# A fused attention and expert kernel: the first transfers in another order, the sink products a tick later, and one copy on another engine

## The chip, the cores and the metric

The kernel runs on one core of a Trainium2 chip. The metric is the device time of one execution in microseconds; three executions of the kernel before took 293.79, 293.94 and 297.29 us, and their median, 293.94 us, is the time before.

## The reference: what is computed

Attention with 4 batches, 8 heads, 768 positions and 64 channels per head, in which a query sees the first 4 positions (the sinks) and the last 128 positions; then a top-1 mixture of 8 experts, each of which serves at most 80 tokens. Cut to what matters:

```
scores = q @ k.T / 8;  keep = (key < 4) | (0 <= query - key < 128)
a = softmax(where(keep, scores, -1e9));  x = (a @ v) as 3072 rows of 512
logits = x @ w_gate;  expert = argmax;  gate_w = softmax(logits)[expert]
for e in 8 experts: keep the 80 tokens of e with the largest gate_w
    out[tok] = gate_w * (relu(x[tok] @ w1[e]) @ w2[e]);  all other rows are 0
```

## The kernel before, in words

**Engines and tiles.** Attention runs in 48 ticks (the loop at L987). A tick handles two units; a unit is one block of 128 queries of one pair of heads. In the first four ticks the units are blocks 0 and 1 of head pairs 0, 1, 2 and 3 of the first batch. TensorE computes the scores (`scores`, L566, matmuls at L581) into one of two PSUM banks, one for each unit, which the next tick uses again. VectorE masks them and takes the maxima (`softmax`, L590: L599, L602, L604, L609). ScalarE takes the exponentials (`exps`, L612: L619) and so frees the bank. GpSimd sorts out the sink columns (`sink_probs`, L622: L627, L628), TensorE turns the probabilities (`transposes`, L635) and the sink columns (`sinks_turn`, L639), ScalarE copies both out (`keep_probs` L646, `sinks_keep` L642), GpSimd cuts the triangles (L654, L661), and TensorE multiplies by the values (`weighted_sinks` L673, `weighted` L687). A tick issues the scores of tick n, the turning of n-1 and the weighted sums of n-2.

**The gate's logits inside the values.** Each head's 64 value columns are followed by 8 columns that hold v times w_gate, so the weighted sum also gives the gate's logits. `value_logits` (L425, matmuls at L433) computes these columns from the turned values `vt` and the gate weights `wg`, and `value_keep` (L436, the copy at L439) writes them into the tile of values `vv`, over zeros that the transfer of `vv` has brought; so it has to come after that transfer. `sink_logits` (L441, L447) and `sink_keep` (L450, L452) do the same for the values of the sinks, from `sv_cols` into `vst_raw`. `round_v` (L412) and `split_v` (L416) then round the sink values for TensorE, one head pair in each of ticks 1 to 4, on VectorE.

**Order.** The ticks are in a hand-written order (`manual_schedule`, L980): each engine executes its instructions in the order of the program text. Work outside the fixed steps is put into named slots by `at(...)` (L875) and comes out at `run(...)`: in a tick, "pe front" comes after the scores and ahead of the turning of the tick before; "pe mid" after the VectorE steps; "act mid" after the exponentials and ahead of `keep_probs`; "pe end" ahead of the weighted sums; "dve end" last, in the order of the `at` calls. One spare PSUM bank (`misc`, L706) is used by turn: the warm-up matmuls of tick 1 (L985), the turned sink columns, then the value logits; each waits until the copy that empties it is done.

**The first transfers.** All are issued by SyncE's queue, in program order. Their sizes are 128 KB for each pair of queries (`first_q`, L467), 132 KB for each pair of keys (`first_k`, L468), 32 KB for `wg`, 256 KB for `sv_cols`, 288 KB for `vst_raw`, 512 KB for `vt`, 576 KB for the first two blocks of `vv`, and 512 KB for the queries of the second group of ticks (`load_q(1)`, L382). Before the change the order is: pair 0 (queries, keys), pair 1, `wg`, `sv_cols`, `vv`, `vt`, pair 2, `vst_raw`, pair 3, `load_q(1)`. GpSimd scales each pair of queries by 0.125 (`scale_first`, L485): pairs 0 and 1 ahead of the ticks, pair 2 in tick 0 and pair 3 in tick 1, each ahead of that tick's `sink_probs`. The queries of the second group are scaled in tick 2 (`scale_q`, L458).

After attention the 24 blocks of tokens are ranked by their gate weights, the rows of the chosen tokens are gathered, and the experts' two matmuls run to the end (L1239, L1260).

Of the kernel before, what the change touches and what calls it, by code (L numbers as in the profile page):

```python
# [26 lines left out]
NPAIR = H // 2  # L27
# [217 lines left out]
def attention_moe(ctx: ExitStack, tc, q, k, v, n_sink, window, w_gate, w1, w2, capacity, q_t, k_t, v_t, vt_t, vs_t, sv_t, wg_t, out):  # L245
    nc = tc.nc
    ve, ac, po, pe = nc.vector, nc.scalar, nc.gpsimd, nc.tensor
# [73 lines left out]
    with ExitStack() as actx:  # L321
# [43 lines left out]
        vst_raw = sm.tile([SROWS, 2, NPAIR, 2 * VD], F32, name="vst_raw", bufs=1)  # L365
# [55 lines left out]
        def load_vt(g):  # L421
            vts[g] = ld.tile([P, NPAIR, 2 * P], F32, tag="vt", name=f"vt_{g}", bufs=1)
            nc.sync.dma_start(vts[g], vt_t[g // NPB, g % NPB])
# [40 lines left out]
        wg = const.tile([P, NPAIR, 2 * E], F32, name="wg")  # L464

        def first_pair(i):
            nc.sync.dma_start(first_q[:, i], q_t[0, 0][:, i])  # L467
            nc.sync.dma_start(first_k[:, i, 0:2 * BLKW], k_t[0][:, i, 0:2 * BLKW])  # L468

        first_pair(0)  # L470
        first_pair(1)
        nc.sync.dma_start(wg, wg_t)
        nc.sync.dma_start(sv_cols, sv_t[0])
        nc.sync.dma_start(vv[0][:, 0:2], v_t[0][:, 0:2])
        load_vt(0)
        first_pair(2)
        nc.sync.dma_start(vst_raw, vs_t[0])
        first_pair(3)
        vst[0], v_done[0] = vst_rows[0], 1
        load_q(1)  # L480
        nc.sync.dma_start(first_k[:, :, 2 * BLKW:4 * BLKW], k_t[0][:, :, 2 * BLKW:4 * BLKW])
# [393 lines left out]
        def at(n, f, *args):  # L875
            cal.setdefault(n, []).append((f, args))
# [51 lines left out]
        at(2, load_v, 0, 3)  # L928
        at((0, "pool"), scale_first, 2)
        at((1, "pool"), scale_first, 3)  # L930
        at((0, "pe end"), sink_logits, 0)
        at((1, "pe end"), sink_keep, 0, ve.tensor_copy)
        for m in range(4):
            at((1 + m, "dve end"), round_v, 0, m, ve.tensor_copy)
            at((1 + m, "dve end"), split_v, 0, m, ve)
        at((1, "pe mid"), value_logits, 0, 0)
        at((1, "pe mid"), value_logits, 0, 1)
        at((1, "act mid"), value_keep, 0)
        for g in range(1, NG):
            n = 4 if g == 1 else 4 * g - 2  # L940
            at((n, "pe front"), value_logits, g, 0)
# [38 lines left out]
        with tc.manual_schedule():  # L980
# [61 lines left out]
            t, i, l = NTK - 1, NTILE - 1, NTILE - 2  # L1042
# [348 lines left out]
```

## Time and profile before

| what | value |
|---|---|
| median of the three executions | 293.94 us |
| profiled execution, its own time | 294.47 us |
| its span, first to last instruction | 292.8 us |
| mean granted TensorE clock | 0.985 of full speed |
| busy share of the span: TensorE matmuls, weight loads | 91%, 74% |
| VectorE, ScalarE, GpSimd | 56%, 58%, 48% |

The profiled execution took 0.53 us more than the median. Of its time 292.8 us lie between the first and the last instruction, and 1.67 us around them. The busy share of TensorE is an average over the whole span; in the first 20 us, which the change touches, TensorE has gaps.

### The profile page before, as it was taken

What the parts mean: (1) busy time and instruction counts of PE and PEld (TensorE: products, weight loads), DVE (VectorE), ACT (ScalarE), POOL (GpSimd) and SP (SyncE); (2) the same over time, 40 slices, a digit from 0 to 9 for tenths busy, and PEclk for the clock granted to TensorE, in tenths of its full rate; (3) what the DMA queues carried; (4) which work ended last, traced back from release to release, by engine and by line L of the source; (5) the groups of instructions that cost most, each with busy time, mean ns of one, the idle gap of its engine ahead of it and who ended that gap; (6) DMA issues with size and microseconds to landing.
All of it is one profiled execution on the core that took longest, in us unless ns stands there. A gap on an engine that the chain in (4) does not pass through costs nothing.

```text
span 292.8 us, 13306 instructions
## 1 busy us (share of the span) xinstructions
PE 266.1 (91%) x5435; PEld 217.9 (74%) x5435; DVE 162.6 (56%) x502; ACT 169.5 (58%) x663; POOL 140.8 (48%) x366
## 2 busy tenths in 40 slices
PE   6699999999999989999989988987979999999991
PEld 2467787777787767777767767555979999999981
DVE  7487858697587968869879888932111011100000
ACT  2377677887868789898989898920102122202220
POOL 4256557755588846657876765847111011011111
PEclk9989999999999999999999999997999999999998
DMA  6997986094964499999999999906996767868501
GB/s 201 318 369 252 320 358 234 3 344 161 341 243 141 130 396 373 344 410 400 354 327 404 324 400 402 386 13 213 281 346 235 255 228 265 296 206 297 181 12 55
DMA packets 30388, 79.18 MB, mean 270 GB/s; under 512 B 3056, under 2 KB 5104, under 8 KB 30320
## 3 DMA queue, kind: packets, MB, share of 16 engines
q1 hardware_dynamic: 29008, 74.85, 71.8%
q0 software_dynamic: 1024, 2.81, 3.3%
q8 instruction: 45, 0.74, 1.0%
q10 hardware_dynamic: 288, 0.60, 0.5%
q14 instruction: 23, 0.19, 0.2%
HBM read 63.46 MB, written 14.78 MB: 267 GB/s over the span
## 4 chain that ended last, share of the span: by engine, by line
PE 55%; ACT 12%; DVE 11%; issue 7%; POOL 7%; DMA 5%; SPq 1%; POOLq 0%; ACTq 0%; DVEq 0%
PE ph L1239 13%; PE py L1260 13%; PE xp L687 7%; PE sc L581 7%; ACT prob L619 7%; PE pp L635 5%; DMA sv_cols<-in_sv_t_dram 4%; PE vw L433 3%; DVE sc L602 3%; DVE nm L609 3%; ACT gts L846 2%; POOL pt L661 1%; DMA xg<-x_rows,idx_in 1%; PE ts L639 1%; PE pry L1298 1%
## 5 line engine op out<-in xcount | busy, mean ns | idle before, releaser
L619 ACT ACTIVATE prob<-sc,nm 128x132 f32<-128x132 f32 (+1 forms) x192 | 69.5, 370 | 21.1 <-DVE nm L609 14.7
L581 PE MATMUL sc<-kv,q 64*64 64x196 f32 (+2 forms) x768 | 45.9, 334 | 4.0 <-ACT prob L619 3.6
L602 DVE COPY_PREDICATED sc<-upper,sc 128x256 f32<-128x256 int8 x80 | 33.8, 423 | 21.9 <-PE sc L581 11.0
L609 DVE TENSOR_REDUCE nm<-sc 128x2 f32<-128x264 f32 (+1 forms) x96 | 41.4, 431 | 3.3
L687 PE MATMUL xp<-kv,pt 128*64 128x72 f32 x752 | 41.0, 229 | 0.7 <-POOL pt L661 0.2
L1300 POOL DMA_INDIRECT out_dram<-y,idx x8 | 7.4, 922 | 65.6 <-ACT y L1299 55.3
L619 ACT ACTIVATION_READ_ACCUMULATOR prob<-sc,nm 128x1 f32 x192 | 38.7, 202 | 0.0
L1223 DVE COPY xs<-px 128x320 f32<-128x320 f32 x8 | 3.9, 492 | 57.0 <-PE px L1221 56.5
L687 PE MATMUL xp<-kv,own 128*64 128x72 f32 x624 | 34.4, 231 | 0.0
L581 PEld LDWEIGHTS sc<-kv,q 64*64 64x64 f32 x768 | 22.4, 133 | 15.4 <-ACT prob L619 9.6
L687 PEld LDWEIGHTS xp<-kv,pt 128*64 128x64 f32 x752 | 31.0, 137 | 3.1 <-POOL pt L661 1.1
L635 PE MATMUL pp<-ident,prob 128*128 128x128 f32 x192 | 31.5, 287 | 0.9 <-ACT pt L646 0.9
L627 POOL CAST stk<-prob 128x32 fp32r<-128x32 f32 x48 | 11.3, 235 | 43.3 <-ACT prob L619 39.3
L1243 ACT ACTIVATE h<-ph 128x320 f32<-128x320 f32 x16 | 7.0, 437 | 38.2 <-PE ph L1239 38.2
L661 POOL TENSOR_SCALAR_AFFINE_SELECT pt<-pt 128x512 f32<-128x512 f32 (+1 forms) x48 | 27.2, 566 | 3.3
L646 ACT COPY pt<-pp 128x512 f32<-128x512 f32 x48 | 28.0, 584 | 0.5 <-POOL own L654 0.5
L654 POOL TENSOR_SCALAR_AFFINE_SELECT own<-pt 128x512 f32<-128x512 f32 (+1 forms) x48 | 27.2, 567 | 0.6 <-ACT pt L646 0.6
L635 PEld LDWEIGHTS pp<-ident,prob 128*128 128x128 f32 x192 | 20.8, 143 | 8.8 <-ACT pt L646 5.3
L687 PEld LDWEIGHTS xp<-kv,own 128*64 128x64 f32 x624 | 25.6, 137 | 2.2
L846 ACT ACTIVATE gts<-krow,under 128x768 bf16<-128x768 f32 x24 | 22.7, 946 | 0.5 <-ACT ex L745 0.2
L1239 PE MATMUL ph<-xs,w 128*64 128x80 f32 x512 | 20.4, 241 | 1.1 <-DVE xs L1223 0.6
L1239 PEld LDWEIGHTS ph<-xs,w 128*64 128x64 f32 x512 | 19.7, 144 | 1.4 <-DVE xs L1223 0.7
(178 smaller groups left out, 510.2 us busy)
## 6 DMA issues: line engine op xcount, KB each, us to landing
w<-in_moe_w_dram SPq DMA_DIRECT2D x16, 1024.0 KB, 8.4
kv<-in_v_t_dram SPq DMA_DIRECT2D x12, 576.0 KB, 7.3
x_rows<-xr SPq DMA_DIRECT2D x22, 292.0 KB, 3.9
vt<-in_vt_t_dram SPq DMA_DIRECT2D x12, 512.0 KB, 7.0
out_dram<-zeros SPq DMA_DIRECT2D x24, 256.0 KB, 7.7
wkv<-in_moe_w_dram SPq DMA_DIRECT2D x6, 1024.0 KB, 8.4
q<-in_q_t_dram SPq DMA_DIRECT2D x11, 512.0 KB, 7.9
kv<-in_moe_w_dram SPq DMA_DIRECT2D x5, 1024.0 KB, 7.8
```

The lines of the kernel that those rows point to most:

```text
L581: pe.matmul(sc[u * D:(u + 1) * D, h, c0 + lo:c0 + hi], qs[g][r, hp, q0:q0 + D], ks[b][r, hp, k0 + lo:k0 + hi], start=True, stop=True, skip ...
L602: ve.copy_predicated(own, upper, sc[:, :, 0:P])
L609: ve.tensor_reduce(out=nm, in_=sc[:, :, lo_c:hi_c], axis=AX.X, op=ALU.max, negate=True)
L619: ac.activation(prob[:, a, h, p0:], sc[:, h, lo_c:hi_c], AF.Exp, bias=nm[:, h:h + 1], scale=1.0, accum_out=ssum[:, n, 2 * hp + h:2 * hp + ...
L635: pe.transpose(st[(t, "pp")][:, a, h], prob[:, a, h, SINK:], ident)
L646: ac.copy(pt, st.pop((t, "pp")))
L654: po.affine_select(out=own[:, a0:], in_=pt[:, a0:], pattern=[[0, 2 - a0], [0, 2], [1, P]], compare_op=ALU.is_ge, fill=0.0, base=0, channel ...
L661: po.affine_select(out=pt[:, a0:], in_=pt[:, a0:], pattern=[[0, 2 - a0], [0, 2], [-1, P]], compare_op=ALU.is_gt, fill=0.0, base=0, channel ...
L687: pe.matmul(xp[m * D:(m + 1) * D, a, h * VD:(h + 1) * VD], pr[:, a, h, m * D:(m + 1) * D], val[:, (2 * hp + h) * VD:(2 * hp + h + 1) * VD] ...
L846: ac.activation(gt, krow[:, c * PIECE:(c + 1) * PIECE], AF.Sign, bias=under[:, i:i + 1], scale=BELOW, accum_out=ra)
L1239: pe.matmul(ph[fc // (HC // 2)][m * D:(m + 1) * D, fc % (HC // 2)], columns(0, e, c, fc * P + m * D), x[:, c], start=(c == 0 and fc % (HC ...
L1260: pe.matmul(to[m * D:(m + 1) * D, dc], columns(1, e, k, dc * P + m * D), h[:, k], start=(k == 0 and (between is not None or dc == 0)), sto ...
```

## The change

Three edits. The queries and keys of pairs 2 and 3 go ahead of `sv_cols`, and `vt` and `vst_raw` go ahead of `vv`, so that `vv` is the last of these thirteen transfers. The sink products of the first batch move from the end of tick 0 to the "pe front" slot of tick 1. The first value logits are copied out by VectorE at the end of tick 1 (behind `round_v` and `split_v` of that tick, by the order of the `at` calls), no longer by ScalarE in its middle.

```diff
-        first_pair(0)
-        first_pair(1)
-        nc.sync.dma_start(wg, wg_t)
+        for i in range(NPAIR):
+            first_pair(i)
+            if i == 1:
+                nc.sync.dma_start(wg, wg_t)
         nc.sync.dma_start(sv_cols, sv_t[0])
+        load_vt(0)
+        nc.sync.dma_start(vst_raw, vs_t[0])
         nc.sync.dma_start(vv[0][:, 0:2], v_t[0][:, 0:2])
-        load_vt(0)
-        first_pair(2)
-        nc.sync.dma_start(vst_raw, vs_t[0])
-        first_pair(3)
...
-        at((0, "pe end"), sink_logits, 0)
+        at((1, "pe front"), sink_logits, 0)
         at((1, "pe end"), sink_keep, 0, ve.tensor_copy)
...
-        at((1, "act mid"), value_keep, 0)
+        at((1, "dve end"), value_keep, 0, ve.tensor_copy)
```

## Rows read from the trace of the kernel before

**Rows 1.** Waits of TensorE from 40 to 200 us: total us, times, longest us.
```profile
PE sv L447 <- DMA sv_cols<-in_sv_t_dram: 0.3, 1, 0.3
```

**Rows 2.** Busy time by stretch: us, length, engines, granted clock, DMA share, GB/s.
```profile
15.00:16.00 1.00, 1.00 (x15) 0.44 (x8) 0.58 (x2) 0.42 (x1) 0.43 (x2) 0.50 0.99 374
...
22.00:24.00 2.00, 2.00 (x46) 1.62 (x38) 1.93 (x5) 1.07 (x6) 1.77 (x6) 1.00 0.17 63
```

**Rows 3.** Chain that ended last, 0 to 40 us: start, length, what.
```profile
3.13 4.10 DMA sv_cols<-in_sv_t_dram
...
11.73 0.41 POOL q L485
...
12.68 0.31 PE ts L639
...
13.32 1.31 PE vw L433 x32
```

**Rows 4.** Transfers issued in 0 to 4 us: size, us from issue to landing.
```profile
kv<-in_v_t_dram SPq DMA_DIRECT2D x1, 576.0 KB, 5.1
```

**Rows 5.** The same view, those issued in 4 to 8.6 us.
```profile
vt<-in_vt_t_dram SPq DMA_DIRECT2D x1, 512.0 KB, 7.0
q<-in_q_t_dram SPq DMA_DIRECT2D x1, 512.0 KB, 7.9
```

**Rows 6.** SyncE's queue in order of time, 0 to 45 us: start, length, transfer.
```profile
3.60 0.43 SPq L474 DMA_DIRECT2D kv<-in_v_t_dram  x1
4.08 0.43 SPq L423 DMA_DIRECT2D vt<-in_vt_t_dram  x1
...
6.93 0.43 SPq L468 DMA_DIRECT2D kv<-in_k_t_dram  x1
7.41 0.43 SPq L382 DMA_DIRECT2D q<-in_q_t_dram  x1
```

**Rows 7.** Instructions in order of time, 0 to 24 us, all engines; idle before in brackets.
```profile
7.37 1.07 PE L447 MATMUL xp<-wg,sv_cols 128*64 128x16 f32 x16 [1.45 <-DMA sv_cols<-in_sv_t_dram]
...
8.19 0.36 ACT L619 ACTIVATE prob<-sc,nm 128x132 f32<-128x132 f32 x1
...
9.13 0.78 PE L581 MATMUL sc<-kv,q 64*64 64x64 f32 x16
...
9.84 0.66 PE L635 MATMUL pp<-ident,prob 128*128 128x128 f32 x4
...
13.01 0.26 ACT L642 CAST stt<-ts 64x128 fp32r<-64x128 f32 x1 [1.46 <-PE ts L639]
...
13.47 0.28 DVE L452 COPY vst_raw<-xp 64x128 f32<-64x128 f32 x1 [1.76 <-DMA vst_raw<-in_vs_t_dram]
...
13.74 0.41 POOL L485 TENSOR_SCALAR q<-q 128x256 f32<-128x256 f32 x1 [1.07 <-DMA q<-in_q_t_dram]
...
13.79 0.51 DVE L412 CAST vst<-vst_raw 64x288 fp32r<-64x288 f32 x1
...
14.67 0.27 ACT L439 COPY kv<-vw 128x128 f32<-128x128 f32 x1 [0.69 <-PE vw L433]
...
15.39 0.49 DVE L599 COPY_PREDICATED_SCALAR sc<-upper,negc 128x256 f32 x1 [0.61 <-PE sc L581]
...
18.10 0.45 DVE L416 TENSOR_TENSOR vst<-vst_raw,vst 32x288 fp32r<-32x288 f32 x1
...
18.87 0.49 DVE L599 COPY_PREDICATED_SCALAR sc<-upper,negc 128x256 f32 x1 [0.32 <-PE sc L581]
```

**Rows 8.** The same view: the later roundings of sink values, and the scaling beside one.
```profile
16.86 1.05 POOL L458 TENSOR_SCALAR q<-q 128x1024 f32<-128x1024 f32 x1
...
17.32 0.75 DVE L412 CAST vst<-vst_raw 64x288 fp32r<-64x288 f32 x1
...
20.80 0.29 DVE L412 CAST vst<-vst_raw 64x288 fp32r<-64x288 f32 x1
```

**Rows 9.** All transfers of values issued at L402: us to landing, least, median, most.
```profile
DMA to landing us min/median/max: 6.7/8.5/12.1
```

## The prediction

> **What bounds the kernel now.** I read the page's busy shares first, then the waits of TensorE, then the chain of waits over the first 40 us, and last the instructions and SyncE's queue in order of time. From 40 to 200 us TensorE waits for a transfer only once, for 0.3 us [rows 1]: there nothing is tied to the clock on the wall, and a tick that starts earlier should end earlier. The first 20 us are different. The chain runs through the sink columns' transfer, then GpSimd's scaling of pair 2 at 11.73, the turned sink columns at 12.68 and the value logits at 13.32 [rows 3]. The exponentials of tick 0 are over at 8.19 + 0.36 = 8.55 [rows 7], so GpSimd could have begun the sink columns then; it stands behind the scaling of pair 2, whose queries land just before 11.73. That is a stall of 3.2 us, and it is what the new order of the transfers removes. The sink products of tick 0 run at 7.37 [rows 7], beside that stall. VectorE meanwhile waits until 13.47 for the sinks' values [rows 7].
>
> **The change, step by step.** The transfers first. They land in the order of issue, roughly as their bytes add up. By the sizes in the text above: 1384 KB, up to and with the values, are down at 3.60 + 5.1 = 8.70 [rows 4, 6]; 1896 KB, with the turned values, at 4.08 + 7.0 = 11.08 [rows 5, 6]; 2444 KB, with the sinks' values, at 13.47, where VectorE's wait for them ends; 2572 KB, with the queries of pair 3, at 13.74, where GpSimd's does [rows 7]; and 3216 KB at 7.41 + 7.9 = 15.31 [rows 5, 6]. I use this curve for the new order, an assumption that the nearest rows carry: the thirteen first transfers are the same set, issued at the same spacing, so SyncE's issues add nothing.
>
> Pairs 2 and 3 then stand at 680 to 1072 KB and are down before 8.70. GpSimd needs pair 2 ahead of the sink columns of tick 0, at 8.55, and pair 3 a tick later. So both scalings (0.41 us each) cost nothing, covered by GpSimd's wait for the exponentials. If pair 2 came later than 8.1, each us would count as before, up to the 3.2 us.
>
> What is late next on TensorE: the scores of tick 1 need the banks that the exponentials free, the second at 8.55; the second half of the 0.78 us [rows 7] puts their end at 8.94. The sink columns' products stand right behind, in front of the turning. Their transfer is at 1328 KB, so down by 8.70, and TensorE does not wait for it; the products cost 1.07 us, now on TensorE's path, to 10.01. The turning takes 0.66 [rows 7], to 10.67, the turned sink columns 0.31 [rows 3], to 10.98, their copy 0.26 [rows 7], to 11.24. The value logits wait for that copy, since it empties the bank, and for the turned values: 1840 KB, 11.1 by the curve. They take 1.31 [rows 3] and end at 12.55. Before they end at 13.32 + 1.31 = 14.63. So TensorE is 2.1 us ahead here.
>
> VectorE does not follow by as much. Its copy of the sink logits waits for the sinks' values, now at 2128 KB: 11.08 + 232/548 of 2.39 = 12.09. The copy 0.28, the rounding 0.51 and the split 0.45 (the duration of the later one) [rows 7] bring it to 13.33, 13.4 with the gaps. Then comes the new work, `value_keep`. Its duration is in no row on this engine: 0.27 on ScalarE, 0.28 for the nearest copy out of PSUM on VectorE with half the partitions [rows 7]. I take 0.28. ScalarE gets 0.27 back, which is worth nothing here, since its next exponentials wait for VectorE's maxima.
>
> The new wait is the point. `value_keep` writes over what the transfer of `vv` brings, and that transfer is now the thirteenth, at 2704 KB: by the curve 13.74 + 132/644 of 1.57 = 14.06. ScalarE did not feel it before, because the values were down at 8.70. So VectorE stands until 14.06 and ends the copy at 14.34. Queued behind it on VectorE are the masks and maxima of tick 2; for those wait the exponentials, and for these the banks of tick 3. TensorE's turned sink columns of tick 1 wait for the same copy, to get the spare bank. The mask of tick 2 starts at 14.36 in place of 15.39 [rows 7]: 1.03 us are left of the 2.1.
>
> From that mask to the one of tick 3, VectorE's own work took 18.10 + 0.45 - 15.39 = 3.16 us; then it waited 0.32 for the scores, to 18.87 [rows 7]. TensorE was slow there: the granted clock was 0.50 between 15 and 16 us [rows 2], the level of 1.2 GHz, after it had stood still from 10.5 to 12.68. In the new order TensorE is done with the value logits 1.5 us before VectorE is ready, so even at that level it has time, and the 0.32 goes. The mask of tick 3 starts at 14.36 + 3.16 = 17.52, 1.35 us earlier. From there the ticks run as before.
>
> Of this, 3.16 has another end. The rounding of tick 2 took 0.75 us at 17.32, beside GpSimd's scaling from 16.86 to 17.91, and 0.29 us at 20.80 [rows 8]. In the new order the scaling starts when its queries land, 15.31, and ends at 16.36, while the rounding starts at about 16.3 (1.93 after the mask, as before). They may just miss each other, which gives 0.46 more. The Trainium skill (SBUF — State Buffer, section Who interferes with whom) says that VectorE's two-port copies and GpSimd share a pair of ports and that the second to issue waits out the first; by this rule the gain would be 1.35 + 0.46 = 1.81 us, and the two roundings quoted agree with it.
>
> **The sum.** 1.35 us off. The profiled execution took 294.47 and would take 293.1; against the median, 0.53 lower, that is 293.94 - 1.35 = 292.6 us. The landing of `vv` can lie between 13.74 and 15.31 by the rows around it, so this case alone runs from a gain of 1.7 to one of 0.1: 292.2 to 293.8.
>
> **Rivals.** (1) The roundings miss the scaling: 1.81 us, 292.1. For it speak the two durations [rows 8]; against it that the estimate of both times is within 0.1 us of an overlap. (2) `vv` is no wait: it lands by 13.4, and VectorE goes on at 13.4 + 0.28 = 13.7, 0.66 earlier than I have it; 2.0 us, 291.9. For it: the values of a later block took at least 6.7 us [rows 9], which from 6.93, the issue of the thirteenth [rows 6], is 13.63. Against: the bytes ahead of it. (3) The gain is given back later: 293.9. It needs a point in the ticks or behind them that depends on a transfer alone. The queue of transfers runs empty in 22 to 24 us [rows 2], so all that was sent in this stretch is down by then, before the ticks use it; that speaks against, and I know of no such point from the rows. But the order of four engines over 44 more ticks can lose a us in small waits. (4) Slower: `value_keep` holds VectorE longer than the removed stall did. The place is the end of tick 1, the price 1 us for each us that `vv` lands after 14.06 + 1.35 = 15.41. The values at L402 took 8.5 us at the median and 12.1 at most [rows 9], which from 6.93 is 15.43 and 19.03. At the middle of the two, 17.2, it costs 1.8: 295.7. Against it: those were sent when larger transfers were ahead of them, and the fourteenth transfer is down at 15.31.
>
> **How the numbers follow.** The forecast has 0.45, (1) 0.15, (2) 0.1, (3) 0.2, (4) 0.1. The time is 292.6; its own range is 292.2 to 293.8. The range from 291.7 to 294.2 holds the forecast and (1) to (3), with 0.2 us for the scatter of the runs, and leaves out (4) and what the small sizes may miss. A measurement of this kernel can tell 2%, 5.9 us, from no change. None of the cases comes near it: the stall itself is 3.2 us, and the far end of (4), 19.03, costs 3.6. So 0.01 for faster by that much, 0.97 for within, 0.02 for slower.
>
> **What would show it.** In the changed profile GpSimd's scaling of pair 2 has no wait behind 9 us; the sink products stand between 8.9 and 10.1; the value logits end near 12.6; VectorE's longest wait in 11 to 15 us is at the copy at L439, for the transfer of the values, until about 14.1; the mask of tick 2 (the third pair's L599) starts at about 14.4 and that of tick 3 near 17.5, and every later tick is 1.3 us earlier. Wrong would be: a wait for the sink columns or the turned values that lasts on TensorE, no wait at L439, one past 15.4, or ticks that start earlier and end at the old time.

## The result, and the profile after

The changed kernel took 295.34 us at the median of 20 executions, the kernel before 294.42 in as many on the same chip: a ratio of 1.0063 [1.0042, 1.0085], some 1.85 us slower by the ratio and 0.92 by the medians. Ratios leave out single executions more than 1.5% above the fastest of their kernel; medians have all. The forecast was 292.6 us, with a range from 291.7 to 294.2, counted from a median of three executions that lay 0.48 below that of the twenty. So the change cost time where a gain of 1.35 us was forecast, and stayed within the 2% to which the prediction gave 0.97. The profiled execution took 296.68 us: 294.5 from its first to its last instruction (before 292.8) and 2.18 around them (before 1.67), at a mean granted clock of 0.978 (before 0.985). On the page TensorE's matmuls are busy for 268.2 us, VectorE for 161.9, ScalarE for 169.1 and GpSimd for 140.0.

First the chain of waits of the changed kernel over the first 40 us (start, length, what). It answers to [rows 3].

```profile
5.51 6.68 DMA vt<-in_vt_t_dram
12.32 1.89 PE vw L433 x32
14.22 1.29 PE sc L580 x12
```

The sink columns and GpSimd's scaling are gone from the chain; a transfer has taken their place, that of the turned values, until 12.19. Then the instructions of the same trace in order of time (start, length, engine, line, what; the idle time before it and what ended it in brackets), which answer to [rows 7, 8].

```profile
1.12 4.86 PE L490 MATMUL sc<-ones_bf 128*128 128x512 bf16 x12 [1.12 <-DVE ones_bf L262]
...
5.96 0.40 POOL L484 TENSOR_SCALAR q<-q 128x256 f32<-128x256 f32 x1 [1.43 <-DMA q<-in_q_t_dram]
...
9.96 1.10 PE L447 MATMUL xp<-wg,sv_cols 128*64 128x16 f32 x16
...
11.79 0.26 ACT L641 CAST stt<-ts 64x128 fp32r<-64x128 f32 x1 [0.93 <-PE ts L638]
...
12.32 1.89 PE L433 MATMUL vw<-wg,vt 128*64 128x16 f32 x32 [0.57 <-DMA vt<-in_vt_t_dram]
...
13.72 0.28 DVE L452 COPY vst_raw<-xp 64x128 f32<-64x128 f32 x1 [2.39 <-DMA vst_raw<-in_vs_t_dram]
...
14.98 0.29 DVE L439 COPY kv<-vw 128x128 f32<-128x128 f32 x1
15.30 0.49 DVE L598 COPY_PREDICATED_SCALAR sc<-upper,negc 128x256 f32 x1
...
16.23 1.04 POOL L458 TENSOR_SCALAR q<-q 128x1024 f32<-128x1024 f32 x1 [1.22 <-DMA q<-in_q_t_dram]
...
17.23 0.29 DVE L412 CAST vst<-vst_raw 64x288 fp32r<-64x288 f32 x1
...
19.35 0.49 DVE L598 COPY_PREDICATED_SCALAR sc<-upper,negc 128x256 f32 x1 [1.34 <-PE sc L580]
```

The scaling of pair 2 is over at 6.36, and GpSimd's stall is gone. Yet the sinks' values land at 13.72 (13.47 in [rows 7]), though 316 KB fewer stand ahead of them, and the mask of tick 2 starts at 15.30 (15.39). `value_keep` at 14.98 waits for no transfer. The mask of tick 3 starts at 19.35, 0.48 later than before, behind a wait of 1.34 us for scores. The first line is TensorE's warm-up ahead of the ticks, twelve matmuls whose results nobody uses. Before the change it read:

```profile
1.12 4.08 PE L491 MATMUL sc<-ones_bf 128*128 128x512 bf16 x12 [1.12 <-DVE ones_bf L262]
```

It took 0.78 us longer this time, and the scores of tick 0, behind it, started at 5.91 in place of 5.13. Third, the granted clock in the same trace (stretch, length, busy time and count of TensorE, its weight loads, VectorE, ScalarE and GpSimd, then granted clock, DMA share, GB/s), which answers to [rows 2].

```profile
13.00:14.00 1.00, 1.00 (x24) 1.00 (x22) 0.28 (x1) 0.23 (x1) 0.85 (x5) 0.50 0.99 394
...
15.00:16.00 1.00, 1.00 (x9) 0.56 (x4) 0.93 (x3) 0.00 (x0) 0.01 (x1) 0.50 1.12 390
...
18.00:19.00 1.00, 1.00 (x22) 0.86 (x22) 0.01 (x1) 0.95 (x4) 0.68 (x4) 0.50 0.95 352
```

The clock column reads 0.60 from 12 to 13 us and 0.50, the level of 1.2 GHz, from 13 to 19 us. Fourth, why the sinks' values came no earlier. The same columns for 6 to 8 us, before the change:

```profile
6.00:8.00 2.00, 0.63 (x12) 0.67 (x12) 1.63 (x5) 0.98 (x5) 0.00 (x0) 1.00 1.01 392
```

and after it:

```profile
6.00:8.00 2.00, 1.44 (x19) 0.54 (x19) 1.44 (x4) 0.46 (x3) 0.36 (x1) 1.00 0.81 212
```

The last two columns matter. The same queue moved 392 GB/s before and 212 after, with the DMA engines busy 0.81 of the time. 180 GB/s less for 2 us is 0.36 MB, about what the new order had saved ahead of the sinks' values (316 KB).

### The profile page after: what moved, and what is told of

Read it like the earlier page. It is cut to its first block, busy times and chain, and to the rows that moved or that the text cites. A ratio compares the mean times of both kernels' runs of the same rounds, so it can differ in the third digit from the quotient of the medians.

```text
span 294.5 us, 13307 instructions
## 1 busy us (share of the span) xinstructions
PE 268.2 (91%) x5435; PEld 219.4 (74%) x5435; DVE 161.9 (55%) x503; ACT 169.1 (57%) x662; POOL 140.0 (48%) x366
## 4 chain that ended last, share of the span: by engine, by line
PE 56%; ACT 11%; DVE 10%; issue 7%; POOL 7%; DMA 7%; SPq 2%; POOLq 0%; ACTq 0%; DVEq 0%
PE ph L1238 13%; PE py L1259 13%; PE xp L686 8%; ACT prob L618 7%; PE sc L580 7%; PE pp L634 5%; PE vw L433 3%; DMA sv_cols<-in_sv_t_dram 3%; DMA vt<-in_vt_t_dram 2%; DVE sc L601 2%; DVE nm L608 2%; POOL pt L660 2%; ACT pt L645 1%; PE px L1220 1%; POOL own L653 1%
## 5 line engine op out<-in xcount | busy, mean ns | idle before, releaser
L618 ACT ACTIVATE prob<-sc,nm 128x132 f32<-128x132 f32 (+1 forms) x192 | 69.4, 369 | 23.3 <-DVE nm L608 13.5
L580 PEld LDWEIGHTS sc<-kv,q 64*64 64x64 f32 x768 | 22.6, 135 | 18.1 <-ACT prob L618 11.1
L1272 ACT COPY yt<-py 128x320 f32<-128x320 f32 x7 | 3.0, 426 | 30.5 <-PE py L1259 30.5
## 6 DMA issues: line engine op xcount, KB each, us to landing
x_rows<-xr SPq DMA_DIRECT2D x22, 292.0 KB, 4.0
```

The costliest lines, as they stand in the source:

```text
L580: pe.matmul(sc[u * D:(u + 1) * D, h, c0 + lo:c0 + hi], qs[g][r, hp, q0:q0 + D], ks[b][r, hp, k0 + lo:k0 + hi], start=True, stop=True, skip ...
L618: ac.activation(prob[:, a, h, p0:], sc[:, h, lo_c:hi_c], AF.Exp, bias=nm[:, h:h + 1], scale=1.0, accum_out=ssum[:, n, 2 * hp + h:2 * hp + ...
```

## The experiments

Fifteen kernels ran. All ratios are to the kernel before, on the same chip, with a 95% interval.

**The changed kernel again, and each edit alone.** The first kernel is the changed one; the other four keep a part of its diff.

```
all_again:  the whole change
order_only: the new order of the transfers alone
sink_only:  at((1, "pe front"), sink_logits, 0) alone
keep_only:  at((1, "dve end"), value_keep, 0, ve.tensor_copy) alone
order_sink: the first two, without the copy on VectorE
```

> The changed kernel once more. It measured 0.6% slower than before, about 1.9 us. If that comes from the first 20 us (theories below), the ticks should again be late by about 0.5 us at tick 3, with the mask of tick 3 at about 19.3 us in place of 18.87, TensorE's granted clock at 0.50 for longer than in the kernel before (there 14.5 to 17.5 us), and the sinks' values landing near 13.6 us. If the step of 1.25 us between ticks 31 and 34 (a wait of 1.2 us for the sink columns of the last batch) is chance, it is not in this trace, and the time is nearer to 1 us than to 2 us slower.

> The new order of the transfers alone. Theory L (late transfers: the pairs of queries and keys, sent ahead, push sink columns, turned values and sinks' values back more than their bytes say): the sink products, still at the end of tick 0, wait on TensorE for the sink columns until about 9.4 us, the scores of tick 1 end near 11.5, and the kernel is slower than the changed one, by 1 us or more over before. Theory V (the copy of the value logits holds VectorE): with the copy on ScalarE, as fast as before or faster. Theory K (TensorE's clock is at the lower level for longer after its gaps): slower by the longer time at 1.2 GHz, with more idle time on TensorE before 13 us than in the changed kernel.

> The sink products in tick 1 alone, transfers and copy as before. Theories L and V: no change within 0.3 us, since GpSimd still waits for pair 2 until 11.7 us and TensorE's sink columns for GpSimd. Theory K: TensorE's gaps lie elsewhere (about 6.7 to 8.6 us, and 10.6 to 12.7), so the clock may fall earlier or for longer, and then the time is up to 1 us off in step with the length of the stretch at 0.50.

> The copy of the first value logits on VectorE alone, transfers and sink products as before. The values are down at 8.7 us, so VectorE does not wait for them; the copy takes about 0.29 us between the split at 14.3 and the mask at 15.39, where VectorE was idle for 0.61 us. Theories L and K: no change within 0.3 us. Theory V: slower by 0.5 to 1.9 us.

> The new order and the moved sink products, with the copy of the value logits back on ScalarE: the changed kernel without its third edit. The runs so far show 2.1 us around the span for both kernels that have the copy on VectorE and 1.75 us for all others, so here 1.75 us are expected. Theory V (the copy holds VectorE inside the span): span shorter than the changed kernel's by 0.3 us or more at the same granted clock. Theories L and K: the same span at the same clock within 0.3 us, so the whole gain over the changed kernel is the 0.35 us around the span.

| kernel | median us | ratio |
|---|---|---|
| all_again | 296.49 | 1.0039 [1.0000, 1.0079] |
| order_only | 299.93 | 1.0136 [1.0082, 1.0190] |
| sink_only | 296.02 | 0.9999 [0.9960, 1.0038] |
| keep_only | 295.36 | 1.0004 [0.9963, 1.0045] |
| order_sink | 295.55 | 1.0059 [1.0031, 1.0088] |

The new order is the edit that costs: the nine measurements of kernels with pairs 2 and 3 sent ahead of `sv_cols`, the first one and those further down among them, gave ratios of 1.0038 to 1.0136. With the sink products moved as well, 1.0136 becomes 1.0059, on another chip and with intervals that overlap at their ends: that the move takes back part of the loss is likely, and how much is not shown. The copy on VectorE changes nothing that this measurement can tell. In order_only, TensorE's products wait for the sink columns with the scores of tick 1 behind them:

```profile
8.97 1.50 PE L447 MATMUL xp<-wg,sv_cols 128*64 128x16 f32 x16 [1.96 <-DMA sv_cols<-in_sv_t_dram]
...
12.63 0.49 DVE L598 COPY_PREDICATED_SCALAR sc<-upper,negc 128x256 f32 x1 [3.79 <-PE sc L580]
```

That mask is the one of tick 1, after VectorE had waited 3.79 us. In the second trace of the changed kernel the same program looks otherwise than in the first:

```profile
12.18 0.28 DVE L452 COPY vst_raw<-xp 64x128 f32<-64x128 f32 x1 [0.22 <-DMA vst_raw<-in_vs_t_dram]
...
13.90 0.29 DVE L439 COPY kv<-vw 128x128 f32<-128x128 f32 x1 [0.62 <-PE vw L433]
...
14.35 0.49 DVE L598 COPY_PREDICATED_SCALAR sc<-upper,negc 128x256 f32 x1 [0.16 <-PE sc L580]
...
17.14 0.49 DVE L598 COPY_PREDICATED_SCALAR sc<-upper,negc 128x256 f32 x1
```

Here the sinks' values are there at 12.18 and the mask of tick 2 starts at 14.35, as forecast. But the kernel with the old order has such executions too, as keep_only shows:

```profile
12.15 0.28 DVE L452 COPY vst_raw<-xp 64x128 f32<-64x128 f32 x1 [0.98 <-DMA vst_raw<-in_vs_t_dram]
13.53 0.29 DVE L439 COPY kv<-vw 128x128 f32<-128x128 f32 x1
13.85 0.49 DVE L599 COPY_PREDICATED_SCALAR sc<-upper,negc 128x256 f32 x1
```

The landing moves by 1.5 us between executions of one order. So one trace on each side can't show a shift of 1.4 us, and the one of before that I took as the base, with the landing at 13.47, lies at the late end.

**The kernel before, again,** without an edit, for that spread.

> The kernel before, once more. Theory P: its sinks' values land in the range of the traces with its order of transfers, 12.2 to 13.5, and its mask of tick 2 starts 1.3 to 2.1 us later; the trace in which the prediction was read was a late one (13.5 and 15.4). If it is typical, both are within 0.3 us of those again. Ratio 1.00 within 0.4%, which shows what this measurement can tell apart.

It measured 1.0036 [1.0000, 1.0072] against itself (294.63 us): ratios of 0.4% say little here. Its landing and mask:

```profile
13.17 0.28 DVE L452 COPY vst_raw<-xp 64x128 f32<-64x128 f32 x1 [1.92 <-DMA vst_raw<-in_vs_t_dram]
...
14.50 0.49 DVE L599 COPY_PREDICATED_SCALAR sc<-upper,negc 128x256 f32 x1
```

Over six traces with the old order the copy at L452 starts at 12.15 to 13.47, mean 12.88, and the mask of tick 2 at 13.83 to 15.49. Over five with the new order in which that transfer still stands behind the turned values and nothing is merged (the changed kernel's two, order_sink, after_warm and after_act_one_more) it is 12.18 to 13.72, mean 12.90, and 13.91 to 15.30. The landing did not move.

The start of the ticks has a spread too: in the sixteen traces with twelve warm-up matmuls ahead of them, these take 4.06 to 5.30 us, and the scores of tick 0 start at 5.11 to 6.35. The trace of the kernel before, with 5.13, lies at the early end.

**Fewer, larger transfers.** Pairs 2 and 3 of the changed kernel as one transfer of queries and one of keys:

```diff
-        for i in range(NPAIR):
-            first_pair(i)
...
+        nc.sync.dma_start(first_q[:, 2:4], q_t[0, 0][:, 2:4])
+        nc.sync.dma_start(first_k[:, 2:4, 0:2 * BLKW], k_t[0][:, 2:4, 0:2 * BLKW])
```

> The changed kernel, with pairs 2 and 3 sent as one transfer of queries (256 KB) and one of keys (264 KB), two issues fewer. Theory S (SyncE issues one transfer in about 0.47 us, so small ones hand out only some 270 KB per us and the engines that move the data run short): in 4 to 8.6 us 1.3 MB or more are moved in place of 1.02 to 1.18 MB, the sinks' values land 0.7 to 1.2 us earlier (11.3 to 12.8 in place of 12.2 to 13.7), and the mask of tick 2 starts earlier by about as much, 13.0 to 14.3. Theory K (the clock alone): landing times and mask as in the changed kernel, 13.9 to 15.3. Time around the span 2.1 us.

295.75 us, 1.0050 [1.0011, 1.0090]. What moved in 4 to 8.6 us, before the change (packets, MB, mean rate, packets below three sizes):

```profile
DMA packets 595, 1.42 MB, mean 309 GB/s; under 512 B 147, under 2 KB 224, under 8 KB 595
```

after it:

```profile
DMA packets 923, 1.10 MB, mean 239 GB/s; under 512 B 214, under 2 KB 733, under 8 KB 923
```

and with the merged transfers:

```profile
DMA packets 862, 1.29 MB, mean 281 GB/s; under 512 B 206, under 2 KB 503, under 8 KB 862
```

Against the first trace of the changed kernel more than half of the lost bytes come back (1.18 MB in its second trace), and in 6 to 8 us the rate is 326 GB/s in place of 212. So the run of small transfers causes the low rate. Merging takes away two issues and a third of the packets under 2 KB at once; which of the two does it is not told apart. The Trainium skill (DMA: Bandwidth & Descriptors, section Rules for kernel authors) says to join many small transfers into one large one; the three rows agree. The sinks' values landed at 12.89 in this trace, within the spread of both orders: that their landing would come earlier is not shown.

**The sinks' values ahead of the turned values,** with the copy on VectorE (swap) and on ScalarE (swap_act).

```diff
+        nc.sync.dma_start(vst_raw, vs_t[0])
         load_vt(0)
-        nc.sync.dma_start(vst_raw, vs_t[0])
...
-        at((1, "dve end"), value_keep, 0, ve.tensor_copy)
+        at((1, "act mid"), value_keep, 0)
```

> The changed kernel with the transfer of the sinks' values (288 KB) ahead of that of the turned values (512 KB). Theory P (the sinks' values are what VectorE waits for, so their place in the queue sets the mask of tick 2): they land 1 to 2 us earlier than in the changed kernel (10.7 to 12.0 in place of 12.2 to 13.7) and VectorE no longer waits for them, or for less than 1 us. The turned values land up to 1 us later and hold TensorE's value logits instead, so the mask of tick 2 starts at 13.5 to 14.6, earlier than 13.9 to 15.3 by 0.5 us in the mean. Rival K (the clock alone): the time follows the granted clock, and the order of these two changes nothing. Around the span 2.1 us.

> The same with the copy of the value logits on ScalarE as before the change. Around the span 1.75 to 1.8 us in place of 2.1, so faster than the kernel above by 0.3 us from that alone. ScalarE then waits for the values at this copy, ahead of its copy of the turned probabilities; if that holds the ticks up, the span is longer than the kernel's above by 0.3 us or more at the same clock.

swap: 296.60 us, 1.0085 [1.0054, 1.0116]; swap_act: 295.91, 1.0038 [1.0001, 1.0075]. In the trace of swap_act:

```profile
10.92 0.27 DVE L452 COPY vst_raw<-xp 64x128 f32<-64x128 f32 x1
...
13.40 1.11 PE L433 MATMUL vw<-wg,vt 128*64 128x16 f32 x32 [1.96 <-DMA vt<-in_vt_t_dram]
...
14.79 0.27 ACT L439 COPY kv<-vw 128x128 f32<-128x128 f32 x1 [2.34 <-DMA kv<-in_v_t_dram]
15.01 0.49 DVE L598 COPY_PREDICATED_SCALAR sc<-upper,negc 128x256 f32 x1 [3.00 <-PE sc L580]
```

The sinks' values no longer hold anything, and the mask is where it was, not at 13.5 to 14.6 as theory P has it: the value logits now wait 1.96 us for the turned values, and the scores of tick 2 stand behind them. The wait for `vv`, until 14.79 here, is real, but falls on ScalarE. In swap the products waited for `sv_cols` until 10.41 and the mask started at 16.13.

**Both waits off TensorE's path, built from these.** Pairs 2 and 3 merged and behind `sv_cols`, the sinks' values ahead of the turned values, the scaling of pair 2 in tick 1, and the value logits behind the scores of tick 2; the second kernel has also fewer warm-up matmuls ahead of the ticks (8 for 12) and more in tick 1 (7 for 3). Of the edit only the slots are shown.

```diff
+        at((1, "pool"), scale_first, 2)
+        at((2, "pe front"), value_logits, 0, 0)
+        at((2, "pe front"), value_logits, 0, 1)
+        at((2, "act front"), value_keep, 0)
```

> A version built on what the traces show: the sinks' values ahead of the turned values, pairs 2 and 3 as one transfer each behind the sink columns, their scaling in tick 1, the sink products in tick 1 as in the changed kernel, and the value logits of the first group in tick 2 behind its scores, copied by ScalarE, as in all later groups. If the sinks' values set the start of the mask of tick 2 (theory S), they land near 11 us and the mask starts at 12.5 to 13.5; the span is 1 us or more shorter than before at the same granted clock, and the time around the span 1.75 us. If the start does not carry to the end (theory G: what the first ticks gain is given back in the stretch from 114 to 131 us, at the sink columns of the last batch), tick 5 is early by 1 us or more but tick 47 is not.

> The version before, with 8 warming matmuls ahead of the ticks in place of 12 and 7 at the start of tick 1 in place of 3, so the same number. The first scores start at about 4.5 us in place of 5.1 to 6.4, and TensorE's gap before the scores of tick 1 is filled. Theory S: a further 0.5 to 1 us earlier at the mask of tick 1, less at that of tick 2, where the sinks' values hold. Theory K: the clock falls less often than in the version before, and the mean granted clock is higher by 0.003 or more.

sinks_first: 294.24 us, 0.9970 [0.9928, 1.0012]; sinks_first_warm: 295.10, 1.0012 [0.9971, 1.0053]. Here the mask of tick 2 does move, to 12.84, earlier than in any trace of either order:

```profile
11.72 0.27 DVE L452 COPY vst_raw<-xp 64x128 f32<-64x128 f32 x1
...
12.84 0.49 DVE L599 COPY_PREDICATED_SCALAR sc<-upper,negc 128x256 f32 x1
```

It is the best version, and its interval lies below the changed kernel's first one, 1.0063 [1.0042, 1.0085], though not below that of all_again; that it beats the kernel before is not shown. What the first ticks gain is in part given back, as theory G has it: the transposes of tick 5 start 1.77 us earlier than in the trace of before, those of tick 31 1.83 and those of tick 47 0.87, and between ticks 31 and 34 TensorE waits 1.0 us for the `sv_cols` of the last batch. In sinks_first_warm the mask came at 12.30, and then TensorE ran dry and its clock fell, so that the transposes of tick 4 started 1.08 us later than before the change. One of its twelve executions took 354.61 us, at a mean granted clock of 0.655, and no trace shows why. The two stretches in the trace:

```profile
20.00:21.00 1.00, 0.11 (x4) 0.12 (x5) 0.99 (x2) 0.00 (x0) 0.93 (x3) 1.00 1.02 411
...
22.00:23.00 1.00, 1.00 (x11) 0.96 (x10) 0.00 (x0) 0.56 (x4) 0.00 (x0) 0.50 0.14 54
```

**The clock.** Matmuls whose results nobody uses, in the gaps of tick 1: 12 more in the changed kernel, 14 in the kernel before (its line is shown). Both write into a PSUM tile that is made larger for it.

```diff
+        at((1, "act front"), fillers, 14)
```

> The changed kernel with 12 more matmuls that compute nothing on TensorE, in its three gaps of tick 1. Theory K (what is lost is TensorE's clock, which falls after the gaps in some executions): the granted clock stays at 1.00 from 12 to 19 us in the trace, as it did in one of the two traces of the changed kernel; the mean granted clock of the runs rises from 0.983 to about 0.99, and their mean span falls by about 1 us. Theories L and V: no gain; the matmuls cost up to 0.3 us where a gap is shorter than they are.

> The kernel before with 14 matmuls that compute nothing in TensorE's gap of tick 1 (10.5 to 12.7 us), while it waits for the sink columns. Theory K: the clock no longer falls at 14 us, the mean granted clock rises from 0.9856 to about 0.99, the mean span falls by 0.5 to 1 us. Theories L and V: no change within 0.3 us.

after_warm: 296.70 us, 1.0114 [1.0059, 1.0168]; before_warm: 295.67, 1.0080 [1.0047, 1.0113]. The mean clock rose to 0.991 in both. before_warm was slower than the kernel before; after_warm was no faster than the changed kernel, whose intervals overlap its own. In before_warm the transposes of tick 5 started 1.57 us earlier than in the trace of before, and the end of TensorE's work was 0.44 later. Between 199 and 245 us TensorE has stops for which the profile shows no cause (total, times, longest):

```profile
PE ph L1247 <- issue: 3.0, 3, 1.3
PE py L1268 <- issue: 0.3, 1, 0.3
```

In the kernel before they were:

```profile
PE ph L1239 <- issue: 1.1, 2, 0.6
PE py L1260 <- issue: 1.0, 1, 1.0
```

That is 3.3 us against 2.1. But the same stops are 1.6 us (order_sink) to 3.5 (swap_act) in the fifteen traces without these fillers, so they are not shown to come from the fillers. Where before_warm loses its time is open.

**The time around the span.** One more small VectorE instruction in the kernel before, and one more small ScalarE instruction in the changed kernel:

```diff
+        ve.memset(half, 0.25)
...
+        at((1, "act mid"), ac.copy, half_a, zeros[:, 0:1])
```

> The kernel before with one more instruction on VectorE at its start (a second fill of one column). If the 0.35 us around the span of the kernels with the copy on VectorE come from one more instruction on that engine, they show here too: 2.1 us around the span in place of 1.75. If they come from the copy itself or its place, 1.75. The span is expected as before within 0.3 us at the same clock.

> The changed kernel with one copy of one column on ScalarE in the place where the copy of the value logits was. ScalarE then has as many instructions as before the change. If the 0.36 us around the span come from ScalarE's one instruction fewer, the time around the span falls from 2.11 to about 1.75 us; if they come from the copy on VectorE, it stays at 2.1. The span is expected as in the changed kernel, 292 to 295.

294.91 us, 1.0017 [0.9983, 1.0052], and 296.61, 1.0081 [1.0037, 1.0126]. The device time less the span is 1.73 us at the mean for the kernel before, 1.80 in the first of these and 2.14 in the second. Over all kernels it is 2.08 to 2.14 where `value_keep` is on VectorE, and 1.72 to 1.82 where it is on ScalarE. So some 0.35 us outside the span come with the third edit. Neither count of instructions is the cause, and no other was found.

## Why the prediction was wrong

**The step that failed** is the first one: "the thirteen first transfers are the same set, issued at the same spacing, so SyncE's issues add nothing". The set was the same, and so was the spacing of the first ten issues (0.47 us; the later ones were up to 0.65 apart in both); the curve of bytes was not. In the new order nine transfers of 32 to 132 KB stand ahead of the first larger one; 128 KB each 0.47 us is 279 GB/s at most, and 733 of the 923 packets of that stretch are under 2 KB (224 of 595 before). In 6 to 8 us eight traces with these transfers kept apart read 187 to 241 GB/s (the five whose landings are given above, order_only, swap and swap_act), and the six of the old order 380 to 407. By bytes alone the sinks' values would have landed at 12.09; the mean was 12.90, against 12.88 in the old order. All of the gain of 1.35 us hung on this. The low rate is shown to come from the small transfers; that it alone set the landing is not, since in the one trace of after_merged the rate was back and the landing (12.89) was not earlier.

**The base.** The gain was counted from one execution, in which the landing was later than in the five other traces of the old order. A mask at 14.36 was close to the changed kernel's (14.35 in all_again), but the old order has it at 13.83 to 15.49 as well. The start of tick 0, which the sum took as fixed at 5.13, varies by 1.24 us too.

**What held.** GpSimd's stall went. The products started at 9.96 (8.94 forecast): the scores ahead of them were late, not `sv_cols`, and 0.78 us of that is the longer warm-up. The value logits started at 12.32, not 11.24: the copy that empties their bank ended at 11.79 + 0.26 = 12.05, 0.81 behind the forecast, as the products were late, and the turned values came last, at 12.19 (11.1 forecast). VectorE took 15.30 - 13.72 = 1.58 us from the landing to the mask, as in rival (2), where it goes on at 13.7, 1.61 after 12.09. "The new wait is the point" was wrong: with the sinks' values this late, `vv` was down before VectorE came to it.

**TensorE after the mask.** "Even at that level it has time, and the 0.32 goes" was wrong in the first trace: the mask of tick 3 came 4.05 us after that of tick 2, with the clock at 0.50 and a wait of 1.34, against 2.79 us in all_again, where the clock stayed at 1.00, and 3.16 forecast. Of the timed executions, 2 of 12 of order_sink had a mean clock of 0.984 or more, against 18 of 26 of the kernel before beside it, and 5 of 11 of all_again against 17 of 27. But fillers that kept the clock up did not make either kernel faster, so the low clock is not shown to be the loss.

The other traces and executions give an estimate of its share. In seven of the seventeen traces the clock column stays at 1.00 from 8 to 60 us. Six of these have spans of 291.8 to 292.2 us, four of them with pairs 2 and 3 sent ahead; the seventh is before_warm, 293.4. In the seven traces with 0.50 for some 6 us or more the span is 293.4 to 296.6, and two of those have the old order; in the three between, it is 291.9 to 294.4. The two traces of the changed kernel, 294.5 and 292.0 us, are one of each kind, and 2.21 of the 2.5 us between them are there at the mask of tick 3. So the low clock goes with a long span under either order; whether it makes it so, or comes with the gaps that do, one cannot tell from that.

Split at a mean clock of 0.984, the mean span of order_sink is 1.2 us longer than that of the kernel before on the same chip in either half (293.85 and 292.62 below it; 293.05, of only two executions, and 291.83 above it), out of 1.65 in all. For all_again it is 0.2 in either half, out of 0.5. By this estimate the clock carries 0.3 to 0.4 us, and the rest is there at like clock. The fillers are no clean test of it: before_warm, at a mean clock of 0.991, has a span 2.4 us longer than the kernel before at 0.984 or more (294.25 and 291.83), so they cost something besides.

**The rivals.** (4), the slower one, had the sign and not the mechanism: VectorE never stood for `vv`, and that its 295.7 is near the 295.34 measured is luck. In (1) the rounding did miss the scaling (17.23, 0.29 us long, against 0.75 in [rows 8]; the scaling ran from 16.23 to 17.27); the Trainium skill (SBUF — State Buffer, section Who interferes with whom) has it that VectorE's two-port copies and GpSimd shut each other out, and the trace agrees. The gain was worth nothing, since the wait of 1.34 us for TensorE covered it. (3) has its point, a wait for a transfer far behind the first ticks, but that is not what the change did: the starts of the transposes, less those in the trace of before, go from +0.85 (tick 5) to +1.97 (tick 47) in the changed kernel's first trace and from -1.06 to -0.67 in its second, and the step lies at tick 31 to 34 in both, where TensorE waits for the `sv_cols` of the last batch:

```profile
PE sv L447 <- DMA sv_cols<-in_sv_t_dram: 1.2, 1, 1.2
```

That wait is 0.3 us in [rows 1] and 0.5 in all_again. Over the traces of the old order it goes from none (keep_only, before_again) to 1.1 us (sink_only), so it varies from execution to execution under either order of the first transfers.

**What makes it slower,** then: about 0.35 of the 1.85 us lies outside the span and comes with the copy on VectorE. The other 1.5 us (0.8 in all_again) comes with the new order, since order_sink has as much without the copy, and sink_only, the moved products without the order, is level. By the split above the clock has a share of 0.3 to 0.4 us in it. In which stretch the rest lies is open: the tick starts of single traces differ by more than that within one kernel.

## What to carry to other kernels

Bytes ahead of a transfer give its landing only while the DMA engines are kept full: read the GB/s and the DMA share of the stretch, and expect a run of small transfers to move less (212 against 392 GB/s here). A wait that is taken off one engine is worth what the next late transfer leaves of it; here the sinks' values, then the turned values, had to leave the path before the mask moved. Before a gain of 1 us is forecast from one trace, know the spread of that moment over several executions of the same kernel: two traces of the changed kernel differ by 1.5 us in the landing on which everything hung.

## What had not been expected of the hardware

- The time outside the span went from 1.73 to 2.11 us when one 0.27 us copy out of PSUM moved from ScalarE to VectorE, in every kernel that has it so.
- Fourteen matmuls of filler in the first 20 us raised the mean clock from 0.986 to 0.991 and the mean span from 292.07 to 294.25 us; where the time goes is open.
- TensorE's stops without a cause in the profile, between 199 and 245 us, come to 1.6 to 3.7 us over the seventeen traces, and the same twelve warm-up matmuls took 4.06 to 5.30 us from trace to trace.
- In sinks_first_warm the low clock came later rather than not at all: 0.50 from 22 to 23 us, behind a stretch in which TensorE was busy for 0.11 of 1 us; before the change it was 0.50 from 15 to 16 us [rows 2].
